# Seven block products for the output of one more group, with the sums of w_out made earlier

## The chip, the cores and the metric

The kernel runs on one core of a Trainium2 chip. The metric is the device time of one execution in microseconds. A core has TensorE (PE in the profile; its weight loads are listed apart as PEld), VectorE (DVE), ScalarE (ACT), GpSimd (POOL) and SyncE (SP), each with an instruction queue of its own that runs in order, and 16 DMA engines that serve transfers issued from SP, ScalarE and GpSimd.

## The reference

Attention with decay over 4 batches, 8 heads, 768 positions and 64 channels, followed by a bilinear feed-forward layer on the 3072 tokens. In the reference a block has 64 positions.

```
for b in range(nb):
    intra = (q_b k_b^T * Dmask) v_b
    inter = (q_b * lam_pow) kv_state
    out_b = intra + inter
    kv_state = lam_block * kv_state + (k_b * rev_pow)^T v_b
x = out as [3072, 512]
y = ((x @ w_a) * (x @ w_b)) @ w_out          # d_model 512, d_ff 1536
```

## The kernel before

The tokens are cut into 24 units of 128 positions (6 units for each batch), and the units into seven groups of 4, 2, 4, 4, 4, 4 and 2 (`GROUPS`; the code counts them from 0, so the third group, units 6 to 9, is `g` = 2, and the fourth, units 10 to 13, is `g` = 3). The feed-forward layer runs group by group. While group g is in it, the attention of group g + 1 is worked in between, at numbered slots: `PLAN[g]` lists (slot, action, unit), `hook(slot)` carries out what stands at a slot, and so the order of instructions in every engine's queue is written out by hand. Nothing is reordered later.

The actions that matter here:

- `P` u (`prep_k`, line 302): GpSimd scales k and q of unit u into `qk` (line 277, one multiplication each), then SP issues a transposing DMA of `qk` into `qkT` for units 10 to 23 (line 311), then the loads of a later unit's q and k are issued on SP (`pump`), then GpSimd issues the load of v (`make_vb`, line 299).
- `S` u (`piece_S`): TensorE makes the scores `kq` from `qkT` (line 344, 8 small matmuls), VectorE masks them into `m` (line 361). `Q` and `O2` make the attention output of two units (line 380), ScalarE copies it into `xT` (line 403), `Q` also makes the scores of further units. `V` updates the state (line 411).
- `sums` (line 535) runs with the last `O2` or `Q` of a group: four sums on VectorE, `xs`, of blocks of the next group's `xT`.
- `TW` i and `TO` j: four sums each on VectorE over blocks of w_a and w_b (`tw`, lines 518 to 521) and of w_out (`two`).
- `G`: a GpSimd copy of one element of the newest `xs` (line 1009). What stands behind it in GpSimd's queue can't start before these sums are done.
- `W`: SP stores a kept output row block of the first two groups (line 786).

In groups with `g` in `S_GROUPS` the first stage (`ffn_seven`) computes the two products with w_a and w_b by block products: for each of six steps i, seven products n = 1, 5, 2, 6, 3, 7, 4 accumulate in three banks `m_q`, `m_r`, `m_p`; ScalarE copies partial results out (line 580), VectorE makes `c11` (599), `c12` (610), `c22` (616) and one half of `ab` (619), GpSimd the other half (612). Product 4 goes into the bank that `c22` is read from. The steps overlap by seven positions of the loop.

The output stage (`ab` times w_out) then has two forms. Plain: for each of the four units 12 matmuls of 512 columns (line 802), a copy out on ScalarE (797) and a store. Seven products (`out_seven`, line 658, for `g` in `O_SEVEN`): 7 × 12 matmuls of 256 columns (line 676), with 12 sums `sm` of blocks of `ab` on VectorE (709 to 715), adds for the two output tiles (742, 770, 772), copies of partial results on ScalarE (694, 778), and one store for each two units (`put`, line 701). It reads the three `two` tiles.

The slots run from 0 to 11 in the first stage and from 12 to 19 in the output stage (12 to 35 in the first group, which has another loop). Slot 0 comes after the first product of a group, before its second.

Tiles live in pools that hand out a fixed number of slots: `wst` (13, for staging, `tw`, `two`, `xs`, `s12`, output tiles), `vb` (8), `o_sb` (4). A tile that finds no free slot waits for the last reader of an old one.

## Time and profile before

| what | us |
|---|---|
| median of three runs | 218.77 (218.74 to 218.99) |
| the profiled execution's own time | 218.79 |
| its span, first to last instruction | 217.1 |
| mean duration of an output matmul, 512 columns (line 802, 159 of them) | 0.347 |
| mean duration of a first-stage matmul, 256 columns (line 565) | 0.255 |
| mean duration of a score mask on VectorE (line 361) | 0.683 |
| mean duration of a sum of w_out blocks (lines 519 to 521) | 0.42 |
| mean duration of a scaling of q on GpSimd (line 277) | 1.043 |
| 14 transposing DMAs, issue on SP (median) | 1.30 |

Matmuls overlap in TensorE, so the duration of one is longer than the distance from one to the next; the chain of waits, which gives a time for so many matmuls in a row, shows the distance. A time in the order of time is the start, then the length, engine, line, operation; in square brackets stands how long the engine had been idle before, and what ended that. A group with `<-` names what is written, then what is read. The chain of waits goes back from the last instruction to what released it each time.

### The profile page before, as it was taken

The page shows a single profiled execution, that of the slowest core. Times are in us where ns is not written, and L with a number is a line of the kernel's source. Part 1 is how long each engine was busy: PE and PEld are TensorE (multiplying, and loading weights), DVE is VectorE, ACT ScalarE, POOL GpSimd, SP SyncE. Part 2 cuts the span into 40 slices and gives each one's busy share as a digit, 9 for nine tenths or more (in the row PEclk, how much of TensorE's full clock was granted, in tenths as well). Part 3 has the DMA queues.
Part 4 walks back from the last instruction along what each step waited for, and adds up shares of the span by engine and source line. Part 5 has one row for each costly group of instructions (what it writes and reads, how often), then busy time and mean ns, then how long its engine had stood idle before and what let it go on. Part 6 is the DMA issues. An engine that isn't in the chain of part 4 may idle for free.

```text
span 217.1 us, 5705 instructions
## 1 busy us (share of the span) xinstructions
PE 210.2 (97%) x2300; PEld 159.6 (74%) x2311; DVE 169.9 (78%) x305; ACT 109.4 (50%) x199; POOL 126.8 (58%) x143
## 2 busy tenths in 40 slices
PE   7799999999999999999999999999999999999994
PEld 2376444556996788755688887788987888989973
DVE  0992995878788587989679899788999787996860
ACT  3686224256872556435465545465535556344522
POOL 6879569984697099992099920699810246300330
PEclk9999999999999999999999999999999999999999
DMA  4999999999799929999999990599900500002302
GB/s 126 301 181 192 203 231 214 229 220 171 111 206 162 161 44 187 180 252 250 231 236 175 186 132 3 128 238 112 107 3 3 193 3 0 0 3 79 117 5 97
DMA packets 84686, 30.78 MB, mean 142 GB/s; under 512 B 71988, under 2 KB 81076, under 8 KB 84660
## 3 DMA queue, kind: packets, MB, share of 16 engines
q1 hardware_dynamic: 51668, 19.86, 45.8%
q0 software_dynamic: 32704, 10.49, 42.8%
q8 instruction: 18, 0.29, 0.6%
q10 hardware_dynamic: 288, 0.07, 0.1%
q14 instruction: 8, 0.07, 0.1%
HBM read 28.32 MB, written 6.29 MB: 159 GB/s over the span
## 4 chain that ended last, share of the span: by engine, by line
PE 92%; DMA 3%; ACT 2%; SPq 1%; issue 1%; DVE 0%; ACTq 0%
PE m_q L565 24%; PE op L802 14%; PE m_r L565 12%; PE o_q L676 7%; PE m_p L565 6%; PE o_ps L380 5%; PE b_ps L488 5%; PE a_ps L488 5%; PE o_r L676 4%; PE kq L344 3%; DMA k<-in_k_dram 3%; PE o_p L676 2%; PE kvd L411 1%; SPq L229 1%; PE tps L322 1%
## 5 line engine op out<-in xcount | busy, mean ns | idle before, releaser
L612 POOL TENSOR_TENSOR ab<-c,c 128x512 bf16<-128x512 bf16 x30 | 34.8, 1167 | 33.9 <-DVE c L610 33.4
L565 PEld LDWEIGHTS <-tw 128*128 128x128 bf16 x576 | 49.1, 98 | 5.9 <-issue 0.3
L565 PE MATMUL m_q<-xs,tw 128*128 128x256 bf16 (+1 forms) x288 | 36.1, 255 | 0.1
L802 PE MATMUL op<-wo_sb,ab 128*128 128x512 bf16 (+2 forms) x159 | 33.2, 347 | 0.7 <-issue 0.3
L361 DVE TENSOR_TENSOR m<-kq,lotri 128x512 bf16<-128x512 f32 x47 | 29.5, 683 | 2.6 <-PE kq L344 2.5
L565 PEld LDWEIGHTS <-wa_sb 128*128 128x128 bf16 x288 | 24.7, 98 | 2.7
L580 ACT COPY s<-m_q 128x512 f32<-128x512 f32 x30 | 17.7, 590 | 16.5 <-PE m_q L565 16.2
L619 DVE TENSOR_TENSOR ab<-c,m_q 128x512 bf16<-128x512 f32 x30 | 20.6, 685 | 6.6 <-PE m_q L565 4.4
L602 POOL TENSOR_TENSOR c<-s 128x512 bf16<-128x512 f32 x7 | 9.3, 1325 | 26.0 <-ACT s L580 26.0
L610 DVE TENSOR_TENSOR c<-u,m_r 128x512 f32<-128x512 f32 x30 | 20.4, 682 | 4.9 <-ACT u L580 4.9
L802 PEld LDWEIGHTS <-ab 128*128 128x128 bf16 x168 | 14.4, 98 | 12.3
L299 POOL DMA_DIRECT2D vb<-in_v_dram x24 | 22.3, 932 | 1.7 <-DMA wo_sb<-in_moe_w_out_dram 1.1
L599 DVE TENSOR_TENSOR c<-s,m_p 128x512 bf16<-128x512 f32 x23 | 15.8, 687 | 7.5 <-PE m_p L565 7.4
L580 ACT COPY s<-m_r 128x512 f32<-128x512 f32 x30 | 17.7, 590 | 7.3 <-PE m_r L565 7.3
L580 ACT COPY u<-m_q 128x512 f32<-128x512 f32 x30 | 17.8, 593 | 6.4 <-PE m_q L565 6.1
L616 DVE TENSOR_TENSOR c<-s,m_q 128x512 f32<-128x512 f32 x30 | 20.6, 686 | 0.5
L277 POOL TENSOR_TENSOR qk<-qf,lp_q 128x512 bf16<-128x512 f32 x18 | 18.8, 1043 | 1.1 <-DMA qf<-in_q_dram 1.1
L403 ACT CAST xT<-o_ps 128x512 bf16<-128x512 f32 x22 | 11.9, 588 | 12.8 <-PE o_ps L380 12.4
L565 PE MATMUL m_r<-xs,tw 128*128 128x256 bf16 (+1 forms) x144 | 18.1, 255 | 0.0
L565 PE MATMUL m_q<-xT,wa_sb 128*128 128x256 bf16 (+1 forms) x144 | 18.1, 255 | 0.0
L565 PE MATMUL m_q<-xT,tw 128*128 128x256 bf16 (+1 forms) x144 | 18.1, 255 | 0.0
L565 PE MATMUL m_p<-xT,wa_sb 128*128 128x256 bf16 (+1 forms) x144 | 18.1, 255 | 0.0
(118 smaller groups left out, 357.7 us busy)
## 6 DMA issues: line engine op xcount, KB each, us to landing
qf<-in_q_dram SPq DMA_DIRECT2D x14, 256.0 KB, 5.1
kf<-in_k_dram SPq DMA_DIRECT2D x14, 256.0 KB, 5.3
vb<-in_v_dram POOLq DMA_DIRECT2D x24, 128.0 KB, 5.5
out_dram<-o_two SPq DMA_DIRECT2D x6, 512.0 KB, 3.0
wa_sb<-in_moe_w_a_dram POOLq DMA_DIRECT2D x6, 256.0 KB, 6.9
wb_sb<-in_moe_w_b_dram POOLq DMA_DIRECT2D x6, 256.0 KB, 7.8
wo_sb<-in_moe_w_out_dram POOLq DMA_DIRECT2D x6, 256.0 KB, 8.0
out_dram<-o_kept SPq DMA_DIRECT2D x6, 256.0 KB, 4.9
```

The lines of the kernel that those rows point to most:

```text
L277: eng_of(eng).tensor_mul(dst.rearrange("p (c b) d -> p b c d", b=2), x[:].rearrange("p (b c) d -> p b c d", b=2), lp.rearrange("p (b c) o ...
L299: nc.gpsimd.dma_start(out=vb, in_=vr[b, nb])
L361: nc.vector.tensor_mul(m, kq[i], lotri_bc)
L488: nc.tensor.matmul(ps[:, lo:hi], lhsT=w_sb[:, s, f * 128:(f + 1) * 128], rhs=xT[:, s, lo:hi], start=(s == 0), stop=(s == KS - 1), skip_gro ...
L565: nc.tensor.matmul(ps[:, f, :], lhsT=w(k, f), rhs=x[:, k, :], start=(first and f == 0 and k == 0), stop=True, skip_group_check=True)
L580: nc.scalar.copy(t, ps)
L610: nc.vector.tensor_add(c12, d["u2"], d["r"])
L612: nc.gpsimd.tensor_mul(ab[:, nf * i:nf * i + nf, 0:h], d["c11"], c12)
L616: nc.vector.tensor_add(d["c22"], d["s5"], d["q"])
L619: nc.vector.tensor_mul(ab[:, nf * i:nf * i + nf, h:2 * h], d["c22"], d["q"])
L676: nc.tensor.matmul(ps[:, t, :], lhsT=x(j, c)[:, t * BLK:(t + 1) * BLK], rhs=w(j)[:, c, :], start=(first and t == 0 and j == js[0] and c == ...
L802: nc.tensor.matmul(op[:, lo:hi], lhsT=ab[:, f, t * 128:(t + 1) * 128], rhs=wo_sb[:, f, lo:hi], start=(f == 0), stop=(f == FC - 1))
```

## The change

The third group's output stage is made by `out_seven` too. The sums of w_out, which stood at slot 15 of the third group, go to slot 22 of the first group (`TO` 0) and slot 0 of the third (`TO` 1, 2), the fifth sum of w_a and w_b (`TW` 4) to slot 7 of the first. A new action `GT` makes GpSimd wait for the last `two`; unit 12 is prepared at slot 1 instead of 3, 13 at 4 instead of 5. The gate `G` goes into the third group's slot 17, and units 15 and 16 are prepared behind it (before: at slots 12 and 14). The scores of unit 13 move from `Q` at slot 13 to slot 14, those of unit 14 stay at slot 18, and those of unit 15 move from slot 19 of the third group to slot 0 of the fourth. The kept rows are stored at slots 3 and 4 instead of 9 and 10. Pools: `wst` 15, `o_sb` 1, `vb` 7, and the tile that the first warming matmuls read is the fourth state buffer, which VectorE clears.

```diff
--- before.py
+++ after.py
@@ -40,32 +40,31 @@
 
 S_GROUPS = (1, 2, 3, 4, 5, 6)
 SUM_ON_VEC = {1: (2,), 2: (0, 1, 2, 3, 5), 3: (1, 2, 3, 4, 5), 4: (1, 2, 3, 4, 5), 5: (1, 2, 4, 5), 6: (0, 1, 2)}
-O_SEVEN = (3, 4, 5)
+O_SEVEN = (2, 3, 4, 5)
 O_EARLY = (5,)
 ACT_COPY = (4, 10, 12, 13, 14, 16, 17, 18, 20, 21)
 FIRST_COPY = (11, 15, 19)
 W_ORDER = ("a0", "a1", "b0", "b1", "a2", "b2", "a3", "b3", "a4", "a5", "b4", "b5", "o0", "q4", "k4", "o1", "v4",
            "q5", "k5", "o2", "v5", "o3")
 PLAN = {
-    0: [(0, "V", 3), (1, "TW", 0), (3, "TW", 1), (5, "TW", 2), (7, "TW", 3),
+    0: [(0, "V", 3), (1, "TW", 0), (3, "TW", 1), (5, "TW", 2), (7, "TW", 3), (7, "TW", 4),
         (9, "P", 4), (9, "L", ("q6", "k6", "o4")), (11, "P", 5), (11, "L", ("o5", "v6", "q7")),
         (12, "L", ("k7", "v7")), (14, "T", 4), (17, "S", 4), (17, "P", 6), (18, "T", 5),
-        (18, "L", ("q8", "k8", "v8")), (21, "V", 4), (22, "S", 5), (22, "LS", 9), (22, "TW", 4), (23, "P", 7), (23, "QS", 8),
+        (18, "L", ("q8", "k8", "v8")), (21, "V", 4), (22, "S", 5), (22, "LS", 9), (22, "TO", 0), (23, "P", 7), (23, "QS", 8),
         (23, "L", ("v9",)), (24, "T", 6), (26, "O2", (4, 5)), (28, "S", 6), (29, "T", 7), (29, "KS", 8),
         (30, "QS", 9), (31, "TW", 5), (33, "KS", 9)],
     1: [(0, "V", 6), (1, "S", 7), (2, "T", 8), (3, "T", 9), (4, "O2", (6, 7)), (4, "P", 10), (5, "S", 8),
         (6, "V", 8), (6, "P", 11), (7, "S", 9), (12, "O2", (8, 9))],
-    2: [(3, "P", 12), (5, "P", 13), (7, "P", 14), (10, "S", 10), (11, "S", 11), (12, "P", 15),
-        (14, "P", 16), (15, "TO", 0), (15, "TO", 1), (15, "TO", 2), (11, "V", 10), (13, "Q", (10, 11, 12, 13)),
-        (14, "V", 12), (16, "O2", (12, 13)), (18, "S", 14), (19, "S", 15)],
-    3: [(1, "P", 17), (4, "P", 18), (7, "P", 19), (17, "G", None), (17, "P", 20)],
+    2: [(0, "TO", 1), (0, "TO", 2), (0, "GT", None), (1, "P", 12), (4, "P", 13), (7, "P", 14), (10, "S", 10), (11, "S", 11),
+        (17, "G", None), (17, "P", 15), (17, "P", 16)],
+    3: [(0, "S", 15), (1, "P", 17), (4, "P", 18), (7, "P", 19), (17, "G", None), (17, "P", 20)],
     4: [(1, "P", 21), (4, "P", 22), (7, "P", 23)],
     5: [(11, "V", 22), (13, "O2", (22, 23))],
 }
-for _g, _u in ((3, 14), (4, 18)):
+for _g, _u in ((2, 10), (3, 14), (4, 18)):
     PLAN[_g] += [(11, "V", _u), (13, "Q", (_u, _u + 1, _u + 2)), (14, "V", _u + 2), (14, "S", _u + 3),
-                 (16, "O2", (_u + 2, _u + 3)), (18, "S", _u + 4), (19, "S", _u + 5)]
-PLAN[2] += [(_s, "W", None) for _s in (9, 9, 9, 10, 10, 10)]
+                 (16, "O2", (_u + 2, _u + 3)), (18, "S", _u + 4)] + ([(19, "S", _u + 5)] if _g > 2 else [])
+PLAN[2] += [(_s, "W", None) for _s in (3, 3, 3, 4, 4, 4)]
 
 
 @with_exitstack
@@ -95,7 +94,7 @@
     PSUM = bass.MemoryType.PSUM
 
     singles = ctx.enter_context(tc.tile_pool(name="singles", bufs=1))
-    wst_pool = ctx.enter_context(tc.tile_pool(name="wst", bufs=13))
+    wst_pool = ctx.enter_context(tc.tile_pool(name="wst", bufs=15))
     ld_pool = ctx.enter_context(tc.tile_pool(name="ld", bufs=4))
     prep_pool = ctx.enter_context(tc.tile_pool(name="prep", bufs=6))
     qkT_pool = ctx.enter_context(tc.tile_pool(name="qkT", bufs=6))
@@ -103,7 +102,7 @@
     xT_pool = ctx.enter_context(tc.tile_pool(name="xT", bufs=2))
     a_pool = ctx.enter_context(tc.tile_pool(name="a", bufs=5))
     ab_pool = ctx.enter_context(tc.tile_pool(name="ab", bufs=2))
-    o_pool = ctx.enter_context(tc.tile_pool(name="o", bufs=4))
+    o_pool = ctx.enter_context(tc.tile_pool(name="o", bufs=1))
     sn_pool = ctx.enter_context(tc.tile_pool(name="sn", bufs=1))
     ps_pool = ctx.enter_context(tc.tile_pool(name="ps", bufs=1, space=PSUM))
     kvps_pool = ctx.enter_context(tc.tile_pool(name="kvps", bufs=1, space=PSUM))
@@ -204,7 +203,8 @@
             load_x(w, u, nc.sync)
             pending.pop(0)
 
-    idle_sb = singles.tile([128, 512], BF16, name="idle_sb")
+    st_bufs = [singles.tile([128, HP, 2, D], BF16, name=f"st{i}") for i in range(4)]
+    idle_sb = st_bufs[3][:].rearrange("p c b d -> p (c b d)")
     nc.vector.memset(idle_sb, 0.0)
     idle_ps = kvps_pool.tile([128, 512], F32, name="idle", tag="kvd")
 
@@ -249,8 +249,7 @@
     nc.gpsimd.memset(bdiag, 0.0)
     nc.gpsimd.memset(bdiag[0:64, 0, :], 1.0)
     nc.gpsimd.memset(bdiag[64:128, 1, :], 1.0)
-    st_bufs = [singles.tile([128, HP, 2, D], BF16, name=f"st{i}") for i in range(4)]
-    for t in st_bufs:
+    for t in st_bufs[:3]:
         nc.gpsimd.memset(t, 0.0)
     tmpe = a_pool.tile([128, NT, H], F32, name="tmpe", tag="a")
     lp_q = singles.tile([128, NT, H, 1], F32, name="lp_q")
@@ -295,7 +294,7 @@
 
     def make_vb(u):
         b, nb = divmod(u, NB)
-        vb = prep_pool.tile([128, H, D], BF16, name="vb", tag="vb", bufs=8)
+        vb = prep_pool.tile([128, H, D], BF16, name="vb", tag="vb", bufs=7)
         nc.gpsimd.dma_start(out=vb, in_=vr[b, nb])
         vbs[u] = vb
 
@@ -1007,6 +1006,9 @@
                 elif name == "G":
                     gate = singles.tile([1, 1], BF16, name="gate")
                     nc.gpsimd.tensor_copy(gate, xs[max(xs)][0:1, 3, 0, 0:1])
+                elif name == "GT":
+                    gate = singles.tile([1, 1], BF16, name="gate")
+                    nc.gpsimd.tensor_copy(gate, two[max(two)][0:1, 3, 0, 0:1])
                 elif name == "W":
                     store_kept()
                 elif name == "T":
```

`out_seven` in the form that the third group takes (not `early`), its order of products and hooks:

```python
product(q, of_x(0, 0), of_w(0, 0), js, True)
product(p, of_x(0, 1), of_w(1, 0), js[:2], True)
last_step()          # the first stage's last product
hook(FC)             # slot 12
product(p, of_x(0, 1), of_w(1, 0), js[2:], False)
hook(FC + 1)
product(r, of_s(0), of_t(0), js, True)
hook(FC + 2)
product(q, of_s(1), of_t(1), js, False)
hook(FC + 3); hook(FC + 4)
product(r, of_s(3), of_w(1, 1), js, False, range(nt // 2))
product(q, of_s(2), of_t(2), js, False)
product(r, of_s(3), of_w(1, 1), js, False, range(nt // 2, nt))
put(u0, o1)
for slot in range(FC + 5, FC + 8):
    hook(slot)
product(q, of_x(1, 1), of_t(3), js, False)
put(u0 + nt, o2)
```

## The prediction

> **What bounds the kernel now.** I read the page first (busy shares and the chain that ended last), then the waits of TensorE, then busy time by stage, then the order of time where one stage goes over into the next, and last the transposes by the DMA engines.

> ```profile
> PE 210.2 (97%) x2300; PEld 159.6 (74%) x2311; DVE 169.9 (78%) x305; ACT 109.4 (50%) x199; POOL 126.8 (58%) x143
> ...
> PE 92%; DMA 3%; ACT 2%; SPq 1%; issue 1%; DVE 0%; ACTq 0%
> ```

> TensorE is busy for 97% of the span and makes 92% of the chain, so time is won or lost where TensorE does less, or stands. It hardly stands at all: its five longest waits sum to 3.0 us, nearly all in the first 13 us, and no DMA is among them.

> ```profile
> PE idle L213 <- DVE idle_sb L208: 1.3, 1, 1.3
> PE tq L871 <- DVE scratch L864: 0.8, 3, 0.4
> PE tk L871 <- DVE scratch L864: 0.4, 2, 0.2
> PE op L802 <- issue: 0.3, 2, 0.2
> PE tn L891 <- ACT scratch L882: 0.2, 1, 0.2
> ```

> By stage (start:end, length, then busy us of TensorE, weight loads, VectorE, ScalarE, GpSimd):

> ```profile
> 72.50:91.60 19.10, 19.10 (x185) 16.54 (x184) 14.85 (x23) 11.33 (x20) 15.53 (x15) 1.00 1.19 149
> 91.60:106.28 14.68, 14.42 (x152) 7.51 (x153) 12.49 (x27) 6.21 (x14) 7.19 (x8) 1.00 1.40 229
> 106.28:124.54 18.26, 18.26 (x173) 16.27 (x170) 14.81 (x23) 11.19 (x20) 15.70 (x15) 1.00 1.27 211
> 124.54:138.09 13.55, 13.55 (x200) 10.97 (x198) 13.41 (x29) 5.26 (x11) 3.21 (x4) 1.00 0.44 58
> ```

> These are the third group's first stage and output stage, then the fourth's. The fourth's output stage is already in the form that the third's will take. It is the model for everything below, its end above all:

> ```profile
> 135.57 0.42 DVE L546 TENSOR_TENSOR xs<-xT,xs 128x512 bf16<-128x512 bf16 x1
> ...
> 136.05 0.18 POOL L1009 COPY gate<-xs 1x1 bf16<-1x1 bf16 x1 [9.88 <-DVE xs L546]
> 136.18 1.03 POOL L277 TENSOR_TENSOR qk<-kf,lp_k 128x512 bf16<-128x512 f32 x1
> ...
> 137.19 1.03 POOL L277 TENSOR_TENSOR qk<-qf,lp_q 128x512 bf16<-128x512 f32 x1
> ...
> 138.09 0.60 PE L565 MATMUL m_q<-xT,wa_sb 128*128 128x256 bf16 x4
> ...
> 138.24 1.29 SPq L311 DMA_TRANSPOSE qkT<-qk  x1
> ```

> The gate lets GpSimd go only when VectorE's sums for the next group are done. The unit behind the gate (20 here) has its transpose issued at 138.24, just after the next group began (138.09). Unit 20 is needed far into that group, so this hurts nobody. How long a transpose takes:

> ```profile
> DMA to landing us min/median/max: 5.2/5.7/7.9
> ```

> [...]at the start: 13 matmuls of 512 columns take 4.70 us (0.36 each), while later 12 of them take 2.59 us in the chain (0.216 each). [...]the sum at 97.56 (line 518) took 0.69 us beside a running GpSimd multiplication, its like 0.42 us when GpSimd was idle. [...]Here all 14 stand in SP's queue.

> **The change part by part**, against the profiled execution's 218.79 us (span 217.1; the median of the runs, 218.77, is the same to 0.02).

> 1. Seven products. Removed: 48 matmuls of 512 columns at 0.216 = 10.4 us. Added: 84 of 256 columns at 0.109 (the chain shows 12 in 1.31) = 9.2 us. Difference 1.2 us. The stages say the same: 14.68 − 13.55 = 1.13, both with four sets of scores. I take −1.13. VectorE gets 12 sums `sm` (0.42 to 0.55 each) and three adds of 0.68, and loses the 12 sums `two`; the model stage carries that load (13.41 of 13.55 us busy) without TensorE waiting.

> 2. The sums of w_out. TO 0 takes TW 4's place at slot 22 of group 0: four instructions for four, 0. TW 4 goes to slot 7, where VectorE is idle 2.16 us before 36.02; it needs 1.55, or some 0.5 more because a GpSimd multiplication runs at 34.57. The product that is late then is read only in group 0's output stage (from 38.3): 0, at worst 0.3. TO 1 and TO 2 at the third group's slot 0: eight instructions, 3.0 us (99.30 to 102.31 in the trace), in a pause of 2.09 us that ends at 74.12. The first `c11` starts at 74.9 instead of 74.1. `c22` of the first step, which TensorE's product 4 at 76.97 waits for, then ends at about 76.85 instead of 76.55. I take +0.1, with 0 and 0.8 (no slack at all) as bounds.

> 3. Gate GT and unit 12 earlier. GpSimd waits until 75 us, scales unit 12 (2 us), issues its v load (0.9), and reaches the first `ab` at 78.1 instead of 75.95. Behind it waits only the third `c12` (81.3), for a buffer of two: 0. SP: the six stores of the first groups move from behind the transpose of 14 to behind 12 and 13; all units up to 14 still have their transposes 6 us or more before their scores: 0.

> 4. Buffers (vb 7, o_sb 1, wst 15, idle_sb in the fourth state buffer): the vb slots that come up were released a group earlier, o_sb is used once now, and GpSimd has one memset less at the start, beside the first loads. 0, bounds −0.1 and +0.3 (a wst slot that waits for a store).

> 5. Units 15 and 16, and the scores of 15. Before: 15 is scaled at 92.97, its transpose is issued at 97.12 behind six stores, lands 7.9 later (105.0), and its scores start at 105.95. After: 15 stands behind the new gate, and its scores stand at slot 0 of the fourth group, right after that group's first product. In the model stage, counted from its first output product: sums done and gate +11.5, scaling done +13.68, transpose issued +13.70 (SP has nothing in front but the store of the first half, free at +13.05), landed +13.7 + L. TensorE arrives after one product, at 138.52, i.e. +13.98; less one set of scores (0.27, four per 16 in 0.55) and eight short inter matmuls (0.1) it is +13.6. The stall is about L. Behind the waiting weight load stands the whole of TensorE's queue, and on it every engine. L is 5.2 to 7.9; the transpose at 143.83, with a 512 KB store issued 2.2 us before as here, took 6.5. Between that and the median of 5.7 I take +6.2. Nothing gives it back: the next stage has TensorE busy 18.26 of 18.26 us. Lost cover: this transpose had 8.8 us before it was needed, now it has none.

> 6. The clock after a stall of 6.2 us. [...](at the start of the trace: 4.70 − 13 × 0.216 = 1.9). Bounds 0 and 2. I take +1.7.

> Sum: 218.79 − 1.13 + 0.1 + 6.2 + 1.7 = 225.7 us.

> **The rivals.** A (likeliest, 225.7): the stall and then the slow clock. B, 224.0: the stall, but the clock holds (218.79 − 1.13 + 0.1 + 6.2). [...]C, the other side, not slower, 217.8 (218.79 − 1.13 + 0.1): the transpose of 15 lands before TensorE comes to its scores. It decides at the gate: it would have to open 6 us earlier, some 5.3 us into the output stage, since GpSimd is idle there (9.88 us before the gate) and only the gate holds it. Against it: the gate reads the fourth group's sums, which can't exist before ScalarE has copied the last attention outputs (+8.7 to +9.8 in the model). D, about 229.5: the transpose collides with the store, the loads of unit 18 behind it and two v loads, and takes 10 us; the longest seen, 7.9, ran behind six stores.

> **How the numbers follow.** A 0.57, B 0.28, C 0.06, D 0.09. The time is A's, 225.7. B with the shortest transpose is 223.0, A with the longest and 2.0 of clock is 227.7; a little beyond both: 222.6 to 228.4. About 0.2% (0.4 us) is what a measurement of this kernel can tell from no change. A, B and D are slower: 0.94. C is faster: 0.05, with 0.01 for what falls between.

> **What would show it.** In the profile after: the third group's output stage about 13.3 us; a wait of TensorE's weight load on the transpose, 5 to 8 us, at about 105, the longest in the list; GpSimd's scaling of 15 at about 103 to 105.5; [...]product 4 of the third group's first step within 0.2 us of 76.97. A transposed unit 15 that has landed by 105, or a score that isn't waited for, would make the prediction wrong; so would a stall under 4 us.

## The result and the profile after

| what | before | after |
|---|---|---|
| median of five runs of each, us | 218.94 (218.74 to 219.15) | 225.74 (225.45 to 227.72) |
| ratio | 1 | 1.0334 (95% interval 1.0288 to 1.0381) |
| the profiled execution's own time | 218.79 | 225.45 |
| its span | 217.1 | 223.2 |
| its mean granted clock of TensorE | 0.998 | 0.985 |

The changed kernel is slower by 6.8 us. The same views are read again, now of the kernel after (its lines carry numbers lower by one). First the page: busy time, the granted clock in 40 slices of 5.58 us, and the engines' shares of the chain.

```profile
PE 211.4 (95%) x2339; PEld 163.8 (73%) x2347; DVE 175.2 (78%) x320; ACT 109.4 (49%) x199; POOL 126.5 (57%) x144
...
PEclk9999999999999999999679999999999999999999
...
PE 84%; issue 5%; DMA 5%; POOL 1%; SPq 1%; DVE 1%; ACT 0%; POOLq 0%
```

TensorE is busy about as long as before (211.4 against 210.2 us) in a longer span: it stands. The 20th and 21st digits of the clock, 106 to 117 us, are the only ones below 9. In the waits of TensorE (sum, times, longest) one line is new:

```profile
PE kq L343 <- DMA qkT<-qk: 5.3, 1, 5.3
PE idle L213 <- DVE st L208: 1.3, 1, 1.3
PE tq L870 <- DVE scratch L863: 0.6, 2, 0.4
```

It stands on top: one wait of 5.3 us of the scores for a transpose. Busy time by stage (the third group's two stages, the fourth's two, columns as in the prediction):

```profile
72.69:91.76 19.07, 19.07 (x185) 16.54 (x184) 16.95 (x30) 11.34 (x20) 15.88 (x16) 1.00 1.26 174
91.76:105.08 13.32, 13.29 (x183) 10.71 (x181) 13.18 (x30) 5.83 (x13) 3.06 (x4) 1.00 0.67 137
105.08:130.78 25.70, 20.43 (x178) 17.36 (x176) 15.32 (x24) 11.62 (x20) 19.80 (x20) 0.87 1.36 190
130.78:144.32 13.54, 13.54 (x199) 10.97 (x197) 13.40 (x29) 5.27 (x11) 3.20 (x4) 1.00 0.45 60
```

Two things stand out. The stage that was changed got shorter, 14.68 to 13.32 us. The stage behind it, whose own matmuls are the same but for one set of scores, went from 18.26 to 25.70 us; TensorE is busy in only 20.43 of it, and the mean clock is 0.87. The order of time where the one goes over into the other:

```profile
102.71 0.42 DVE L545 TENSOR_TENSOR xs<-xT,xs 128x512 bf16<-128x512 bf16 x1
...
103.19 0.18 POOL L1008 COPY gate<-xs 1x1 bf16<-1x1 bf16 x1 [9.93 <-DVE xs L545]
103.33 1.03 POOL L276 TENSOR_TENSOR qk<-kf,lp_k 128x512 bf16<-128x512 f32 x1
...
104.33 1.03 POOL L276 TENSOR_TENSOR qk<-qf,lp_q 128x512 bf16<-128x512 f32 x1
...
105.08 0.60 PE L564 MATMUL m_q<-xT,wa_sb 128*128 128x256 bf16 x4
...
105.39 1.30 SPq L310 DMA_TRANSPOSE qkT<-qk  x1
...
110.95 0.61 PE L343 MATMUL kq<-qkT 64*128 64x128 bf16 x8 [5.27 <-DMA qkT<-qk]
```

GpSimd stands 9.93 us before the gate and is let go at 103.2; two scalings of 1.03 us later SP issues the transpose of unit 15 at 105.39. TensorE has made the group's first product by 105.68, and the scores of 15 are next in its queue. The chain of waits gives the transfer itself:

```profile
105.39 5.52 DMA qkT<-qk
```

Issued at 105.39, landed 5.52 later, scores at 110.95. The clock around this, by stretches (of the last three columns the first is the granted clock, the second the DMA share, the third GB/s):

```profile
105.68:107.97 2.29, 0.01 (x1) 0.00 (x0) 0.00 (x0) 0.68 (x2) 2.27 (x3) 1.00 0.89 220
107.97:110.95 2.98, 0.00 (x0) 0.00 (x1) 0.00 (x0) 0.00 (x0) 1.23 (x2) 0.50 1.61 180
110.95:114.79 3.84, 3.84 (x24) 2.72 (x25) 1.29 (x2) 1.64 (x3) 0.70 (x1) 0.50 1.57 224
114.79:118.21 3.42, 3.42 (x33) 3.06 (x32) 2.61 (x4) 1.88 (x4) 3.42 (x4) 1.00 0.96 242
```

Between 105.68 and 110.95 nothing runs on TensorE, and the clock falls to 0.50 at 107.97, 2.3 us into the pause, not at its end. It stays there until 114.79, so 3.84 us of work run at half speed: 24 matmuls, where at full speed 33 take 3.42 us. Half of the 3.84, 1.92 us, is an estimate of what the slow clock costs.

### The profile page after: what moved, and what is told of

It reads as the page before. It is cut to its first block, busy times and chain, and to the rows that moved or that the text cites. A ratio compares the mean times of both kernels' runs of the same rounds, so it can differ in the third digit from the quotient of the medians.

```text
span 223.2 us, 5802 instructions
## 1 busy us (share of the span) xinstructions
PE 211.4 (95%) x2339; PEld 163.8 (73%) x2347; DVE 175.2 (78%) x320; ACT 109.4 (49%) x199; POOL 126.5 (57%) x144
## 4 chain that ended last, share of the span: by engine, by line
PE 84%; issue 5%; DMA 5%; POOL 1%; SPq 1%; DVE 1%; ACT 0%; POOLq 0%
PE m_q L564 24%; PE m_r L564 12%; PE op L801 9%; PE o_q L675 7%; PE m_p L564 6%; PE b_ps L487 5%; PE a_ps L487 5%; PE o_ps L379 4%; PE o_r L675 4%; DMA k<-in_k_dram 3%; DMA qkT<-qk 2%; PE kq L343 2%; PE o_p L675 2%; SPq L229 1%; PE tps L321 1%
## 5 line engine op out<-in xcount | busy, mean ns | idle before, releaser
L564 PE MATMUL m_q<-xs,tw 128*128 128x256 bf16 (+1 forms) x288 | 36.6, 257 | 0.0
L579 ACT COPY s<-m_r 128x512 f32<-128x512 f32 x30 | 17.7, 590 | 13.3 <-PE m_r L564 13.3
L801 PE MATMUL op<-wo_sb,ab 128*128 128x512 bf16 (+2 forms) x114 | 22.1, 335 | 0.4 <-issue 0.2
L675 PEld LDWEIGHTS <-sm 128*128 128x128 bf16 x192 | 17.5, 98 | 3.6 <-DVE sm L714 0.4
L564 PE MATMUL m_r<-xs,wb_sb 128*128 128x256 bf16 (+1 forms) x144 | 18.4, 258 | 0.0
```

The source lines that it names most:

```text
L564: nc.tensor.matmul(ps[:, f, :], lhsT=w(k, f), rhs=x[:, k, :], start=(first and f == 0 and k == 0), stop=True, skip_group_check=True)
L579: nc.scalar.copy(t, ps)
L675: nc.tensor.matmul(ps[:, t, :], lhsT=x(j, c)[:, t * BLK:(t + 1) * BLK], rhs=w(j)[:, c, :], start=(first and t == 0 and j == js[0] and c == ...
L801: nc.tensor.matmul(op[:, lo:hi], lhsT=ab[:, f, t * 128:(t + 1) * 128], rhs=wo_sb[:, f, lo:hi], start=(f == 0), stop=(f == FC - 1))
```

## The experiments

The theory: the loss is one of order. The scores of unit 15 stand in TensorE's queue at a point where their transpose can't have landed yet, and the clock falls in the pause; the seven products themselves gain about 1.1 us. Rivals: the seven products, the moved sums or the fewer buffers cost time of their own. Each edit is against the changed kernel, if not said otherwise. The kernel before has medians of 218.85 to 218.88 us beside these runs.

**The scores of 15 later in the fourth group.** First from slot 0 to slot 6, then to slot 2 (the two added lines, one for each kernel).

```
-    3: [(0, "S", 15), (1, "P", 17), ...
+    3: [(6, "S", 15), (1, "P", 17), ...
+    3: [(2, "S", 15), (1, "P", 17), ...
```

> The changed kernel with the scores of unit 15 at slot 6 of the fourth group instead of slot 0; nothing else differs. Theory A (order: the scores stand in TensorE's queue before their transpose can land, and the stall halves the clock): the stall of 5.3 us and the 1.9 us of slow clock both go, the gain of the seven products stays: 217.8 us, 1.0 under the kernel before, no wait of TensorE on the transpose. Theory B (load: the new output stage and the moved sums overload VectorE and GpSimd, and the stall is only where it shows first): most of it comes back as another wait, 222 us or more.

> The changed kernel with the scores of unit 15 at slot 2 of the fourth group: TensorE has six more products of 0.44 us (2.6 us) in front of them. Theory A: the wait falls from 5.3 to about 2.7 us, [...]so the 1.9 us of slow clock go too: 220.9 us. If the clock falls all the same: 222.8. Theory B: as the changed kernel, 225 or more.

Slot 6 gave 219.42 us (ratio to before 1.0035, 1.0018 to 1.0052); there is no wait for a transpose any more, and its span is 216.7 us. Slot 2 gave 222.08 (1.015, 1.0118 to 1.0183) with this in the order of time of its profiled execution (221.23 us, clock 1.000; in two of the other five the mean clock was 0.992):

```profile
111.25 0.40 PE L343 MATMUL kq<-qkT 64*128 64x128 bf16 x8 [2.16 <-DMA qkT<-qk]
```

Less distance, more wait: 0 us at slot 6, 2.16 at slot 2, 5.27 at slot 0. So the order makes the loss. That the clock would hold at slot 2 was the author's estimate; by the mean clock it held in four executions of six. But slot 6 didn't reach the 217.8 us that was expected. The stages of its profile (the fourth group's two) and one line of its order of time show a part of what is missing:

```profile
104.81:123.83 19.02, 18.89 (x178) 16.39 (x176) 14.84 (x24) 11.34 (x20) 18.94 (x20) 1.00 1.42 215
123.83:137.85 14.02, 13.71 (x199) 10.88 (x197) 13.84 (x29) 5.27 (x11) 4.00 (x5) 1.00 0.70 115
```

```profile
124.74 1.05 PE L675 MATMUL o_q<-wo_sb,ab 128*128 128x256 bf16 x8 [0.31 <-POOL ab L611]
```

GpSimd is busy 18.94 of 19.02 us (15.70 of 18.26 before): the preparation of 15 and 16, which the gate pushes out of the third group, is now made in the fourth, and GpSimd's last halves of `ab` come late for the output stage. With the moved scores (0.27) taken off, the first stage has 0.49 us more than before and the output stage 0.47: 0.96 us. That GpSimd is the cause is tested further down (GpSimd relieved).

**The order alone, without the seven products.** The kernel before, with the gate ahead of 15 and 16, and the scores of 15 at slot 0 of the fourth group.

```
-    2: [..., (12, "P", 15), (14, "P", 16), ..., (18, "S", 14), (19, "S", 15)],
-    3: [(1, "P", 17), ...
+    2: [..., (17, "G", None), (17, "P", 15), (17, "P", 16), ..., (18, "S", 14)],
+    3: [(0, "S", 15), (1, "P", 17), ...
```

> The kernel before, with units 15 and 16 prepared behind the gate at slot 17 and the scores of unit 15 at slot 0 of the fourth group; the output stage stays plain and the sums stay where they were. Theory A: scaling done about 2.1 us after the sums (103.95), transpose issued at about 106.2, landed at 111.7, TensorE there at 106.5: stall 5.2 and slow clock 1.9: 226 us. Theory B: no new load, so 219 us.

Measured: 226.68 us (1.0354, 1.0339 to 1.037), mean clock 0.985. Its order of time:

```profile
106.66 1.23 SPq L311 DMA_TRANSPOSE qkT<-qk  x1
...
112.13 0.61 PE L344 MATMUL kq<-qkT 64*128 64x128 bf16 x8 [5.23 <-DMA qkT<-qk]
```

The same wait (5.23 against 5.27) in a kernel that has neither seven products in this stage nor moved sums nor changed buffers. The whole loss is there, and 0.94 us more. The 0.94 is not a clean measure of the seven products, though: here 4.92 us of work ran at half speed (112.13 to 117.05) instead of 3.84, which costs 0.54 us more, while the changed kernel has 0.55 us more outside its span (see the last experiment). The two nearly cancel.

**The wait kept, the clock held.** Ahead of the scores at slot 0, 23 matmuls of 512 columns into a bank that nobody reads.

```
-    3: [(0, "S", 15), ...
+    3: [(0, "F", 23), (0, "S", 15), ...
+                elif name == "F":
+                    fill = ps_bank("fill", [128, 512], F32)
+                    for _ in range(us):
+                        nc.tensor.matmul(fill, lhsT=wa_sb[:, 0, 0:128], rhs=wb_sb[:, 0, 0:512], ...)
```

> The changed kernel with 23 matmuls of 512 columns (5.0 us at full clock) in front of the scores of unit 15, whose results nobody reads: TensorE works through the wait instead of standing. The transpose lands when it did. If the slow clock is a price of its own: 225.5 less 1.9 = 223.6, matmuls of 0.109 us behind the scores, and runs that differ less among themselves. If the matmuls behind the wait are slow for another reason (feeding buffers, VectorE): as the changed kernel, 225.5.

Measured: 223.22 us (1.0202, 1.0189 to 1.0215), clock 1.000. The scores start at 110.59 instead of 110.95, so the wait is filled and hardly shortened (22 of the 23 matmuls are in the trace):

```profile
105.53 5.13 PE L1015 MATMUL fill<-wb_sb,wa_sb 128*128 128x512 bf16 x22
...
110.59 0.40 PE L343 MATMUL kq<-qkT 64*128 64x128 bf16 x8
```

The fourth group's first stage takes 23.65 us instead of 25.70. That is 2.05 us, of which 0.14 is the filling being shorter than the pause (5.13 against 5.27): the clock is worth 1.9 us by the stage, the same as half of the 3.84 us of work at half speed. By the medians the difference is 2.5, some 0.3 of it outside the span.

**What the gate is for.** With the scores at slot 6, unit 15 prepared in the output stage again and only 16 behind the gate; then both in the output stage and no gate (again an added line for each).

```
-        (17, "G", None), (17, "P", 15), (17, "P", 16)],
+        (12, "P", 15), (17, "G", None), (17, "P", 16)],
+        (12, "P", 15), (14, "P", 16)],
```

> The version with the late scores (slot 6), and unit 15 prepared at slot 12 of the third group, ahead of the gate; unit 16 stays behind it. Theory: the late version missed 217.8 because GpSimd, which took over 6 us of preparation for 15 and 16 after the gate, has its halves of ab ready late at the end of the fourth group (TensorE waits 0.3 us for them, and more in the runs that took longer). With one unit less behind the gate GpSimd is 3 us ahead there: 218.3 us and runs closer together. Rival: the two multiplications now meet VectorE's sums in a stage where VectorE has no pause, and cost as much as they free: 219.4 or more.

> As before, but units 15 and 16 both without the gate, at slots 12 and 14 of the third group, scores of 15 at slot 6 of the fourth. If the gate earns its place, four GpSimd multiplications of 1.03 us hold up VectorE's sums by up to 4 us in a stage where it is busy 13.3 of 13.3 us, and TensorE waits for sm: 220 to 222 us. If the gate is needless: 217.8.

With 15 early: 219.85 us (1.0042, 1.0029 to 1.0054), as its rival expected. The wait for `ab` in the fourth group is gone, and TensorE waits in the third group's output stage instead, 0.83 + 0.34 us for VectorE. Without the gate: 223.63 (1.0233, 1.0212 to 1.0253), more than the 220 to 222 expected, since here the clock falls too: its mean is 0.983 to 0.992 in every run. The order of time without the gate:

```profile
95.68 3.37 DVE L710 TENSOR_TENSOR sm<-sm,ab 128x512 bf16<-128x512 bf16 x2
...
96.37 1.05 POOL L276 TENSOR_TENSOR qk<-kf,lp_k 128x512 bf16<-128x512 f32 x1
97.38 1.04 POOL L276 TENSOR_TENSOR qk<-qf,lp_q 128x512 bf16<-128x512 f32 x1
...
99.70 2.83 PE L675 MATMUL o_r<-two,sm 128*128 128x256 bf16 x12 [3.44 <-DVE ab L618]
```

and the same sums with the gate (the kernel with the scores at slot 6), where GpSimd stands still:

```profile
94.11 0.75 DVE L710 TENSOR_TENSOR sm<-sm,ab 128x512 bf16<-128x512 bf16 x2
```

Two sums of VectorE take 3.37 us beside GpSimd's multiplications and 0.75 without them; by the instructions one by one it is the first of the two that takes 3.04 us, from 95.68 to 98.72, and GpSimd's multiplications end at 98.42. That it is the multiplications that hold the sum is read from these times (the last section has more of them), not tested apart. In an output stage of seven products VectorE is busy 13.18 of 13.32 us, so there is no slack to take this up: TensorE waits 3.44 us, and the clock falls to 0.50 at 99.70.

**What the moved sums are for.** With the scores at slot 6, `TO` 1 and `TO` 2 in the output stage, and so without the gate `GT`.

```
-    2: [(0, "TO", 1), (0, "TO", 2), (0, "GT", None), (1, "P", 12), ...
+    2: [(12, "TO", 1), (12, "TO", 2), (1, "P", 12), ...
```

> The version with the late scores, and the last eight sums of w_out back in the third group's output stage (slot 12) with no GT gate. They take 3.0 us of VectorE in a stage without a pause there: if moving them was what made room, 222 us, TensorE waiting for sums; if they were hidden anyway, 219.4 as with the late scores.

Measured: 223.38 us (1.0191, 1.0163 to 1.0218). Eight sums of 0.42 us fill VectorE from 95.5 to 98.5, and TensorE waits 2.81 us for `sm` behind them. The busy times of the pause and of a stretch after it:

```profile
96.70:99.50 2.80, 0.01 (x1) 0.00 (x0) 2.73 (x8) 0.36 (x1) 0.00 (x0) 1.00 0.00 0
...
101.00:103.00 2.00, 2.00 (x18) 1.23 (x17) 1.34 (x3) 1.09 (x3) 0.00 (x0) 0.50 0.00 0
```

By the waits the pause is 2.81 us, and 0.6 us after it the clock falls to 0.50. By the mean clock it fell in three of the four runs (223.25 to 223.57 us); the one in which it held took 221.86 us.

**The seven products alone.** With the scores at slot 6, the third group's output stage in the plain form.

```
-O_SEVEN = (2, 3, 4, 5)
+O_SEVEN = (3, 4, 5)
-    wst_pool = ... bufs=15
+    wst_pool = ... bufs=14
-    o_pool = ... bufs=1
+    o_pool = ... bufs=3
```

> The version with the late scores, and the third group's output stage plain again (48 matmuls of 512 columns; wst 14 and o_sb 3 slots). The seven products are worth 1.1 us by the stages: 219.4 + 1.1 = 220.5 us. If VectorE's load in that stage took part of it back, less: 219.5 to 220. It also shows whether the half microsecond by which time and span differ more in the changed kernel comes with the seven products.

Measured: 221.21 us (1.0108, 1.0094 to 1.0122). As a whole this doesn't compare: with 14 `wst` slots TensorE waits 0.85 us in the third group's first stage for a copy that itself waits for a store to give its slot free, and the stage takes 20.08 us instead of 19.07. The output stage by itself takes 14.28 us against 13.34 with seven products: 0.94 us for them. Time beyond the span is 2.0 to 2.3 us here too.

**GpSimd relieved.** With the scores at slot 6, the first `c11` of the fourth group on VectorE; then also k of unit 17 scaled on VectorE (the second pair of lines, the second kernel only).

```
-SUM_ON_VEC = {..., 3: (1, 2, 3, 4, 5), ...
+SUM_ON_VEC = {..., 3: (0, 1, 2, 3, 4, 5), ...
-        make_ks(u, "dve" if u < n0 + 4 else "pool")
+        make_ks(u, "dve" if u < n0 + 4 or u == 17 else "pool")
```

> The version with the late scores, and the fourth group's first c11 added on VectorE instead of GpSimd. If GpSimd's 6 us of late preparation are what the late version still pays (0.5 us in the first stage, 0.47 at the head of the output stage of the fourth group), 1.3 us less on GpSimd there takes most of it back: 218.5 us, no wait of TensorE on ab, runs closer together. If it is VectorE or chance: 219.4, as with the late scores.

> The same with the k of unit 17 also scaled on VectorE, which has a pause there: GpSimd another 1.0 us ahead. By the GpSimd theory as before or a little better, 218.2 to 218.5; [...]

Measured: 218.25 us over 22 runs (218.04 to 220.30; ratio 0.997, 0.9955 to 0.9986), and with unit 17 as well 218.31 (0.9975, 0.9961 to 0.999), nothing more. In the first one's fourth group no wait for `ab` is left:

```profile
105.57:124.20 18.63, 18.63 (x179) 16.39 (x176) 15.65 (x25) 10.93 (x19) 18.55 (x19) 1.00 1.49 219
124.20:137.74 13.54, 13.54 (x200) 10.97 (x197) 13.40 (x29) 5.26 (x11) 3.13 (x5) 1.00 0.78 118
```

TensorE is busy without a gap in both stages: 18.63 and 13.54 us against 19.02 and 14.02. So GpSimd's backlog was what slot 6 still paid. This kernel beats the one before by 0.3% (a small gain, but the interval leaves out 1) and the changed one by 3.3%.

**Time outside the span.** The kernel before with only the merging of `idle_sb` into the fourth state buffer, to see whether that adds time ahead of the first or behind the last instruction.

```
-    idle_sb = singles.tile([128, 512], BF16, name="idle_sb")
+    st_bufs = [...]          # moved up from below
+    idle_sb = st_bufs[3][:].rearrange("p c b d -> p (c b d)")
...
-    for t in st_bufs:
+    for t in st_bufs[:3]:
```

> The kernel before with one edit of the change alone: the tile that the first warming matmuls read is the fourth state buffer, cleared by VectorE. By the sum it costs nothing: 218.9. If it is what makes time and span differ by half a microsecond more in the changed kernel: 219.4.

Measured: 218.93 us (0.9992, 0.9972 to 1.0013), 1.68 to 1.75 us outside the span, as before. So the time outside the span does not come from the merging.

## Why the prediction was right

It gave 225.7 us, by its rival A, the stall and then the slow clock; 225.74 was measured. The stall, its place and the slow clock behind it are all in the trace, so the mechanism is right and not only the number. By its steps:

1. Seven products, −1.13: right. The output stage went from 14.68 to 13.32, of which 0.27 is a set of scores that moved out, so −1.09 from the products. The kernel with the plain form says −0.94 (by stages).
2. Sums of w_out, +0.1: nothing to be seen. The first stage takes 19.07 us instead of 19.10; `c11` of the third group started at 75.03 (predicted 74.9), and product 4 at 77.13, which with the stage starting 0.19 us later is on time (predicted within 0.2 us of 76.97). `TW` 4 in the first group did come late: the sum ahead of it took 1.95 us instead of 0.42 beside a GpSimd multiplication, where some 0.5 us more had been allowed for such a meeting. VectorE's next product for `ab` started at 36.97 instead of 36.02, and the output stage behind it still takes 14.70 us, as argued: the cost was mis-sized, but it met slack.
3. The gate GT and unit 12, 0: right; no wait of TensorE in that stage.
4. Buffers, 0: right within the bounds. The 0.19 us by which the third group starts later are there by 38 us: the 13 matmuls at the start take 5.09 us instead of 4.70. These are the warming matmuls, and the trace has the clock at full speed from 5.57 us instead of 4.78 in this execution. Nothing points to a buffer.
5. The stall, +6.2: right in its place and mechanism, too large by 0.9. It was 5.27. Two terms were mis-sized. About 0.7 is L, the time from issue to landing: 5.52, where a transpose behind a store had been taken as the model and 6.2 chosen between that and the median of 5.7. A store was issued at 104.35, 1 us ahead, and no delay by it is seen. Most of the rest is TensorE, which was through its first product at 105.68, +13.92 from the stage's start, where +13.6 had been worked out; this shortens the wait. The issue (105.39) came at +13.63, predicted +13.70.
6. The clock, +1.7: right that it falls, and near in size: 1.9 us by the stage (25.70 − 18.26 − 0.27 − 5.27) and by the filled kernel. How likely the fall was had been the author's estimate; the trace before has no pause of that length (its longest wait of TensorE is 1.3 us). The mean clock was 0.985 in all five executions of this kernel and all four with the order alone: it fell every time. The last section has the falls as the traces show them.

With the later start these steps sum to −1.09 + 0.16 + 5.27 + 1.9 = 6.2 us, by which the end of the fourth group moved (138.09 to 144.32); the span grew by 6.1. The profiled execution grew by 6.66: 0.55 us more lies outside the span (time less span is 1.65 to 1.75 before and 2.2 to 2.4 after). The prediction had no step for it, and no view shows what it is. It is there in the other kernels that come from the changed one too (2.0 to 2.4), and not in the two that come from the one before (1.7 to 1.8). It was tried on the merged buffer and on the plain output stage, and is neither; it stays open. So the hit to 0.04 us is partly luck: a stall too large by 0.9 stood against 0.55 us outside, a clock dearer by 0.2 and a start later by 0.2.

Rival B, the clock holds, 224.0, is what the filled kernel brings about: 223.22 us (with the measured stall and the time outside, B would be 224.0 − 0.9 + 0.55 = 223.6). Rival C, the transpose has landed, 217.8: slot 6 is this case for TensorE, and gave 219.42. What C left out is the backlog on GpSimd, 0.96 us, and the 0.55 outside: 217.8 + 0.96 + 0.55 = 219.3. The prediction put the preparation of 15 and 16 behind the gate (2 us of GpSimd for k and q of each unit, and the issue of the v loads) at nothing in the fourth group. That held only because TensorE itself stood and waited for the transpose; with that wait gone, GpSimd is late next. Rival D, 10 us for the transfer, didn't come.

## What to carry to other kernels

When a gate pushes the preparation of data behind a point, follow the data to its reader: gate, scaling, issue and landing (here 7.7 us together, 103.2 to 110.9) must fit before the first instruction that reads it, and if that instruction stands in an engine's ordered queue, it belongs as many slots later, or everything behind it waits too. A gain in one stage, here 1.1 us, is real and yet worth nothing while the order behind it costs seven (5.3 of wait and 1.9 of clock); moving one entry of the plan turned +6.8 us into +0.5, and moving one sum off the engine that was then late turned that into −0.6. If a wait can't be moved, its price here had two parts, the wait and the clock after it, and the second (1.9 us) was bought back with matmuls whose result nobody reads (223.22 us instead of 225.74, clock 1.000).

## What the runs showed of the hardware

**When the clock falls.** In the four traces in which the clock falls in mid-run, from 1.00 to 0.50, the fall and the rise stand 3.41 us or twice that apart: 107.97 and 114.79 in the changed kernel, 110.22 and 117.05 with the order alone, 100.15 and 103.56 with the sums late, 99.70 and 103.11 without the gate. In the traces of before and after, the fall also comes a whole number of such steps after the first record of the full clock: 30 steps in the changed kernel (5.57 to 107.97), and 62 in the kernel before (4.78 to 216.41, behind its last matmul). The steps ahead of a fall in the changed kernel and in the one with the sums late, and the step with most of the pause of the slot 2 kernel, in which the clock held (found by counting such steps on from its first record of the full clock, 5.09 us):

```profile
104.55:107.97 3.42, 1.14 (x11) 0.78 (x8) 0.97 (x2) 1.07 (x2) 3.40 (x4) 1.00 0.72 193
96.73:100.15 3.42, 0.63 (x6) 0.58 (x7) 3.28 (x9) 0.33 (x1) 0.00 (x0) 1.00 0.00 0
107.49:110.90 3.41, 1.60 (x14) 1.07 (x11) 1.34 (x2) 1.54 (x3) 3.40 (x4) 1.00 1.34 160
```

**VectorE beside GpSimd.** The size: 3.37 us for two sums beside two multiplications, 0.75 us without. The form, by the times: the sum ends just after the multiplication. In the changed kernel, for the sum of step 2:

```profile
33.64 1.95 DVE L520 TENSOR_TENSOR tw<-wa_sb,tw 128x512 bf16<-128x512 bf16 x1
34.23 1.06 POOL L276 TENSOR_TENSOR qk<-qf,lp_q 128x512 bf16<-128x512 f32 x1
```

The sum ends at 35.59, 0.29 us after the multiplication. In the traces of before and after, six sums of `sm`, `tw` or `two` took 0.69 to 1.95 us beside a multiplication, and each ended 0.28 or 0.29 us after it; so did the three without the gate from 93.76 to 98.72 us, which took 0.81, 1.26 and 3.04 us and ended 0.28 to 0.30 us after one. It also goes the other way. In the traces of before and after, three sums that began 0.25 to 0.32 us ahead of a multiplication took 0.42 us, and the multiplication ended 0.90 to 0.94 us after them. A multiplication that began 0.49 us behind a sum without the gate took 1.22 us instead of 1.04, and one 0.48 us behind a sum with 15 early took 1.23. What is not shown is why two sums that began 0.59 us (here) and 0.69 us (without the gate) ahead of a multiplication were held all the same; the profile's times on GpSimd are rough.
